# Query feature sums ahead of one more copy on the vector engine, their transposes issued as items of their own

## The chip, the cores and the metric

The kernel runs on one core of a Trainium2 chip. The metric is the device time of one execution in microseconds (us), as the median of several runs. A core has five engines that each work through their own instructions in order and wait for each other through semaphores: TensorE (PE, matmuls; PEld is its weight load), VectorE (DVE), ScalarE (ACT), GpSimd (POOL) and SyncE (SP, which here issues nearly all DMAs).

## The reference

Two attention branches share one input x of 2048 rows and 640 columns (32 heads of 20) and are mixed by a gate per row.

```python
g = sigmoid((x * gate_w).sum(-1, keepdims=True))
return g * A(x) + (1 - g) * B(x)
```

Branch A is linear attention with softmax features. Branch B cuts the rows into four segments of 512. In each it takes causal softmax attention within the segment and adds, by a weight per head, a read of a memory that all earlier segments have filled:

```python
phi = lambda t: jnp.where(t > 0, t + 1.0, jnp.exp(t))
for s in range(4):
    a_dot = softmax(qs @ ks.T * scale + mask) @ vs
    pq = phi(qs)
    a_mem = (pq @ M) / (pq @ z + 1e-6)
    outs.append(g * a_mem + (1 - g) * a_dot)
    pk = phi(ks)
    M, z = M + pk.T @ vs, z + pk.sum()
```

The features phi(q) of the queries are what the change is about. Segment 0 needs none, since the memory is empty.

## The kernel before, in words

The first 144 us compute branch A up to its normalised rows and the projections of segment 0 for branch B. The rest of the kernel is branch B and the output product. All five engines are on a manual schedule there: the order in which the code emits instructions is the order on each engine, and the order is written out by hand.

**Steps.** The loop over `dstep` makes 16 steps, four to a segment; "step s.d" is step d of segment s, each counted from 0. A step treats two groups of four heads, a and b. It emits five *bursts*: a burst is eight matmuls into two PSUM tiles `st_ps` (L621), each turned into probabilities `PT` by an exponential on ACT (L625), and then masked on POOL by triangular selects (L632). Between the bursts the step emits *items*, a list that the strings in `PLAN` spell out, one letter per item:

- `h`: half a projection (five matmuls, L804, into a PSUM tile `proj`, and a DVE copy, L810) of keys, queries or values of the next segment. After the second half of a key or query chunk follow its transpose on SP (L520) and an entry in the list of features to come.
- `f`, `o`: half an output row block (`f`) or half of branch A's part of one (`o`): matmuls L755 into a `proj` tile and a DVE copy into `orow` or `oTA` (L766).
- `A`, `D` and `B`, `C`: the products of probabilities and values (L677) into the PSUM tile `nda`, `A` and `D` for group a of this step, `B` and `C` for group b of the step before. `D` and `C` end with the memory read (L685), the memory update (L690) and the epilogue `emit_epi` on DVE and POOL: `rec` (L702, L704), `td` (L714; L710 in segment 0), `mtmp` (L720), then on POOL `oB` (L717), `Msb` (L723) and `Mbd` (L724).
- `x`, `y`: the sums that finish one chunk of features, `x` for keys, `y` for queries.
- `t`, `u`: transposes of finished rows on SP.

An item is emitted when the work of the items so far falls behind the share of the bursts; items of no weight, such as `x` and `y`, go with the item before them.

**Features.** phi is made in two parts. `exps` (L780) takes the exponential on ACT into `ek`, after the first burst for queries and after the third for keys. `rest` holds the sums: on DVE a minimum with 1 in place (L783) and the sum with max(x, 0) (L784). For keys that is all. For queries the sum goes to one staging tile `phiq_st` (a part of a tile that the profile calls Eq), and two transposes on SP (L789) follow at once, which bring it into place in `xTf`.

**Buffers that matter here.** `proj` has two PSUM banks that all halves (`h`, `f`, `o`) take in turn: a half can begin when the copy of the half before last has ended. `nda` has one buffer: `A` and `B` begin after the epilogue of the group before. `st_ps` has two tiles, `ek` two buffers, `phiq_st` one.

**Order in a step of segment 2**, as the string `hhBhhyCfhhxADt` gives it: two key halves, `B`, two query halves, the query sums with their transposes (`y`), `C` with its epilogue, an output half, two value halves, the entry `x`, `A`, `D`, a row transpose.

Of the kernel before, what the change touches and what calls it, by code (L numbers as in the profile page):

```python
# [15 lines left out]
def kernel(  # L16
# [15 lines left out]
    nc = tc.nc  # L32
    P = 128
# [266 lines left out]
    for n in range(KC):  # L300
        emit_foldM(WkT, WkA, n)
        if n in (1, 3):
            for sc in (n - 1, n):
# [4 lines left out]
                          in_=gw_ps[:, :, None, None].to_broadcast([P, KC, 2, 1]))  # L308
# [15 lines left out]
    for n in range(KC):  # L324
# [10 lines left out]
        out=xg, in0=vA[:, :, 0, 320].rearrange("p (g u) -> p u g", u=4)[:, :, :, None].to_broadcast([P, 4, 4, 4]),  # L335
# [192 lines left out]
    for ch in range(NCH):  # L528
# [8 lines left out]
        part, c = (("k", ch // 4), ("q", ch // 4), ("v", ch // 4), ("v", 4 + ch // 4))[k]  # L537
# [33 lines left out]
    with ExitStack() as bctx:  # L571
# [16 lines left out]
        xr = xTf.rearrange("p (r u) -> p r u", u=L)  # L588
        HOMES = {1: ((0, 6, 0), (6, 8, 1)), 2: ((0, 3, 9), (3, 8, 2)), 3: ((0, 6, 0), (6, 8, 1))}
        phiq_st = Eqf[:, 2 * G * L:2 * G * L + 2 * L].rearrange("p (h e) -> p h e", e=32)  # L590
# [44 lines left out]
        def bursts(a, b):  # L635
            out = []

            def add(name, parts, at):
                PT = bpt.tile([P, 4, L], BF16, name=name)

                def burst():
                    by_pairs = at if name == "PT1" and parts[0][0].last else ()
                    emit_burst(parts, PT, by_pairs)
                    if not by_pairs:
                        triangles(PT, at)
                out.append(burst)
                return PT

            for st in (a, b):
                st.PT[0] = add("PT0", ((st, 0, 0),), (0,))  # L650
                st.PT[1] = add("PT1", ((st, 3, 384), (st, 1, 0)), (0, 3))
                if st is a:
                    PT = add("PT2", ((a, 2, 0), (b, 2, 256)), (0, 2))
                    a.PT[2], b.PT[2] = (PT, 0), (PT, 256)
            return out
# [13 lines left out]
        def pv_items(st, js):  # L669
            vB = vBs[st.s % 2]  # L670

            def piece(j, i):
                if j == 0 and i == 0:
                    st.nda = bnd.tile([P, 2, 512], F32, name="nda")
                nd = st.nda[:, 0, 0:4 * GP].rearrange("p (j i e) -> p j i e", j=4, i=4)
                for c in range(j + 1):
                    nc.tensor.matmul(nd[:, j, i], lhsT=block(st, c)[:, i, (j - c) * P:(j - c + 1) * P],  # L677
                                     rhs=vB[:, c, 4 * st.g + i, :], start=(c == 0), stop=(c == j))
            return [(0.026 * (j + 1), lambda j=j, i=i: piece(j, i)) for j in js for i in range(4)]

        def mem_items(st):
            g = st.g

            def am(j):
                nc.tensor.matmul(st.nda[:, 1, j * GP:(j + 1) * GP], lhsT=phiq_block(st.s, g, j),  # L685
                                 rhs=Mbd[:, g].rearrange("p i e -> p (i e)"), start=True, stop=True)

            def mz(c):
                Mz = st.nda[:, 1, 4 * GP:5 * GP].rearrange("p (i e) -> p i e", i=4)
                nc.tensor.matmul(Mz, lhsT=phiks[st.s % 2][:, c, 4 * g:4 * g + 4, :],  # L690
                                 rhs=vBs[st.s % 2][:, c, 4 * g:4 * g + 4, :],
                                 start=(c == 0), stop=(c == 3))
            return ([(0.037, lambda j=j: am(j)) for j in range(4) if st.s > 0]
                    + [(0.037, lambda c=c: mz(c)) for c in range(4) if st.s < NSEG - 1]
                    + [(0.0, lambda: emit_epi(st))])
# [30 lines left out]
        def emit_oT(ch):  # L726
            oT = bw.tile([P, KC, P], BF16, name="oT", bufs=4)
            nc.sync.dma_start_transpose(out=oT, in_=oBs[ch // 4][:, ch % 4])
            oTs[ch] = oT
# [40 lines left out]

        waiting = {"k": [], "q": []}
        sums = {"k": [], "q": []}

        def features(part, sc):
            src = stages[part][sc % 2][:, :, 0:DH]
            dst = phiks[(sc // 4) % 2][:, sc % 4] if part == "k" else phiq_st

            def exps():
                ek = bw.tile([P, H, DH], BF16, name="ek")
                nc.scalar.activation(out=ek, in_=src, func=ACT.Exp)  # L780

                def rest():
                    nc.vector.tensor_scalar_min(out=ek, in0=ek, scalar1=1.0)  # L783
                    nc.vector.scalar_tensor_tensor(out=dst[:, :, 0:DH], in0=src, scalar=0.0,  # L784
                                                   in1=ek, op0=ALU.max, op1=ALU.add)
                    if part == "q":
                        c = sc % 4
                        for g0, g1, r in HOMES[sc // 4]:
                            nc.sync.dma_start_transpose(  # L789
                                out=xr[:, r:r + 4 * (g1 - g0 - 1) + 1:4, c * P:(c + 1) * P],  # L790
                                in_=phiq_st[:, 4 * g0:4 * g1].rearrange("p h e -> p (h e)"))
                sums[part].append(rest)
            waiting[part].append(exps)

        def run_first(fns):
            if fns:
                fns.pop(0)()
# [19 lines left out]
        def half_items(s, order):  # L817
            return [half_item(part, 4 * s + c, half) for part, c in order for half in range(2)]
# [9 lines left out]

        PLAN = {0: ("hhhhhhxAhD", "hhBhyhChoxAoD", "hoBhoyChoxAoD", "hoBooyCooxAoD"),
                1: ("hhBhhyChhxADtt", "hhBhhyCfhhxAD", "hhBhhyCfhhxADt", "hhBhhyCfhhxAD"),
                2: ("hhBhhyCfhhxADt",) * 4,
                3: ("fBfyCffADtt", "ftBfCftfAD", "fBfCftfAD", "ufBfCfffAD")}

        oT4 = oTA[:, 0:4]

        def turn_last(n):
            nc.sync.dma_start_transpose(out=oT4[:, n, 0:3], in_=oBs[NSEG - 1][:, n, 0:3 * P])

        prev = None
        for dstep in range(NSEG * G // 2):
            s, gd = divmod(dstep, G // 2)
            if gd == 0 and s + 1 < NSEG:
                halves = half_items(s + 1, FIRST_SEG if s == 0 else CHUNKED)
            a, b = Step(2 * dstep), Step(2 * dstep + 1)
            items = []
            for w in PLAN[s][gd]:
                if w in "hfo":
                    items += {"h": halves, "f": fins, "o": aouts}[w].pop(0)  # L850
                elif w in "xy":
                    items.append((0.0, lambda part="kq"[w == "y"]: run_first(sums[part])))
                elif w == "u":
                    items += [(0.0, lambda n=n: turn_last(n)) for n in range(4)]
                elif w == "t":
                    items.append((0.0, lambda ch=turns.pop(0): emit_oT(ch)))
                else:
                    st = a if w in "AD" else prev
                    items += pv_items(st, (0, 1, 2)) if w in "AB" else pv_items(st, (3,)) + mem_items(st)
            share = sum(w for w, _ in items) / 5  # L860
            done = 0.0
            for n, burst in enumerate(bursts(a, b)):
                burst()
                if n in (0, 2):
                    run_first(waiting["kq"[n == 0]])
                while items and (n == 4 or done + items[0][0] / 2 < (n + 1) * share):
                    w, fn = items.pop(0)
                    fn()
                    done += w
            prev = b  # L870
# [93 lines left out]
```

## Time and profile before

| what | value |
|---|---|
| median of 3 runs | 344.57 us (344.26 to 344.86) |
| the profiled execution | 343.32 us |
| its span in the profile | 341.6 us |
| PE busy | 316.6 us, 93% |
| ACT busy | 259.9 us, 76% |
| DVE busy | 222.7 us, 65% |
| POOL busy | 206.4 us, 60% |
| granted TensorE clock | 1.00 |
| steps of segment 0 | 143.8 to 188.2 us |
| steps of segment 1 | 188.2 to 235.5 us |
| steps of segment 2 | 235.5 to 283.7 us |
| steps of segment 3 and the end | 283.7 to 341.6 us |

The page of the profile gives busy time by engine, and in 40 equal slices of the span, where each digit is the busy share in tenths (9 is 90% or more). The table of waits names for each engine and line the idle time before it and the event that came last before it began: total us, times, longest. The event is inferred; where the engine named had long been done, it was another. A timeline lists instructions in order of time: start in us, duration in us, engine, line, operation, output, input, size, how many were merged, and in brackets the idle time of the engine before, with what ended it. The ends of matmuls are modelled.

### The profile page before, as it was taken

To read this page: it belongs to the slowest core of one execution; us is meant where nothing else is said; L and a number is where in the kernel's file an instruction comes from. 1 tells how busy PE (TensorE), PEld (TensorE's weight loads), DVE (VectorE), ACT (ScalarE), POOL (GpSimd) and SP (SyncE) were. 2 spreads that over 40 slices of the span, in tenths; PEclk is the share of its full clock that TensorE was granted. 3 is DMA by queue.
4 is the path that set the end of the run, shared out by engine and by line. 5 is a ranking of instruction groups with operands and counts; after the bars stand their busy time and mean duration, and the time that the engine had idled before them with its cause. 6 is when DMAs were issued, how large, how long until landed. Compare 5 with 4: busy or idle time off the path is not lost.

```text
span 341.6 us, 9744 instructions
## 1 busy us (share of the span) xinstructions
PE 316.6 (93%) x4021; PEld 218.8 (64%) x4021; DVE 222.7 (65%) x448; ACT 259.9 (76%) x331; POOL 206.4 (60%) x301
## 2 busy tenths in 40 slices
PE   7999999989969999889988999999999999999994
PEld 6788888874437777645555556565555556665672
DVE  2466886479779889547676568667565664544552
ACT  4888887508855345699999988898888889889842
POOL 8177688500407888846566666757666666666550
PEclk9999999999999999999999999999999999999999
DMA  8839969895006778854433373543664551431222
GB/s 237 268 72 180 120 97 116 124 306 187 0 2 60 98 125 119 140 98 87 54 63 64 41 113 75 74 91 63 111 77 84 109 86 49 90 79 46 40 80 77
DMA packets 83381, 34.21 MB, mean 100 GB/s; under 512 B 69258, under 2 KB 83338, under 8 KB 83338
## 3 DMA queue, kind: packets, MB, share of 16 engines
q1 hardware_dynamic: 82906, 33.11, 52.6%
q8 instruction: 31, 0.51, 0.7%
q10 hardware_dynamic: 432, 0.49, 0.5%
q14 instruction: 12, 0.10, 0.1%
HBM read 9.21 MB, written 2.62 MB: 35 GB/s over the span
## 4 chain that ended last, share of the span: by engine, by line
PE 47%; ACT 21%; DVE 17%; issue 7%; POOL 5%; DMA 3%; SPq 0%; ACTq 0%; DVEq 0%; POOLq 0%
ACT PT L625 18%; PE st_ps L621 7%; PE pk L214 6%; PE pv L214 6%; PE proj L755 5%; PE proj L804 4%; PE nda L677 4%; PE pq L265 4%; PE proj L506 3%; DVE tt L454 3%; DVE Eq L784 3%; PE num L410 2%; DVE rr L432 2%; DVE td L714 2%; DVE zz L251 2%
## 5 line engine op out<-in xcount | busy, mean ns | idle before, releaser
L625 ACT ACTIVATE PT<-st_ps 128x1024 bf16<-128x1024 f32 x160 | 154.1, 1024 | 19.2 <-PE st_ps L621 11.7
L632 POOL TENSOR_SCALAR_AFFINE_SELECT PT<-PT 128x512 bf16<-128x512 bf16 (+1 forms) x130 | 84.9, 671 | 51.7 <-ACT PT L625 51.4
L226 POOL TENSOR_TENSOR EkSn<-Ek,krec 128x1280 bf16<-128x1280 bf16 x16 | 37.7, 2362 | 18.0 <-DVE krec L225 16.3
L677 PEld LDWEIGHTS <-PT 128*128 128x128 bf16 x1280 | 39.9, 96 | 12.0 <-issue 7.3
L677 PE MATMUL nda<-vB,PT 128*128 128x21 bf16 x1280 | 42.8, 173 | 1.6 <-DVE mtmp L720 1.2
L810 DVE CAST Z<-proj 128x320 bf16<-128x320 f32 x48 | 22.9, 488 | 32.2 <-PE proj L804 32.0
L804 PEld LDWEIGHTS <-xTf 128*128 128x128 bf16 x320 | 28.0, 97 | 21.5 <-issue 12.8
L214 PEld LDWEIGHTS <-xTf 128*128 128x128 bf16 x320 | 35.3, 113 | 7.1 <-ACT xTf L192 0.3
L222 DVE TENSOR_REDUCE ksum<-Ek 128x64 f32<-128x1280 bf16 x16 | 23.6, 1478 | 12.4 <-ACT Ek L218 12.4
L270 ACT ACTIVATE Eq<-pq 128x1024 bf16<-128x1024 f32 x20 | 19.4, 1021 | 13.0 <-PE pq L265 13.0
L454 DVE TENSOR_TENSOR tt<-num,rr 128x640 f32<-128x640 f32 x32 | 25.2, 813 | 5.2 <-PE num L410 2.7
L755 PE MATMUL proj<-WkA,oTA 128*128 128x320 bf16 x160 | 27.3, 299 | 0.0
L621 PE MATMUL st_ps<-Z 32*128 32x512 bf16 (+3 forms) x256 | 23.4, 299 | 4.2 <-ACT PT L625 2.1
L545 POOL TENSOR_TENSOR oA<-tt 128x640 bf16<-128x640 f32 x16 | 24.6, 1544 | 4.0 <-DVE tt L454 3.2
L218 ACT ACTIVATE Ek<-pk 128x640 bf16<-128x640 f32 x32 | 20.8, 701 | 7.8 <-PE pk L214 5.4
L717 POOL TENSOR_TENSOR oB<-td 128x320 bf16<-128x320 f32 x23 | 19.8, 862 | 11.4 <-DVE td L714 8.4
L410 PEld LDWEIGHTS <-Eq 128*128 128x128 bf16 x384 | 20.2, 96 | 9.4 <-issue 5.7
L621 PE MATMUL st_ps<-Eq 32*128 32x512 bf16 (+3 forms) x256 | 24.5, 299 | 1.8 <-ACT PT L625 0.9
L214 PE MATMUL pv<-WvA,xTf 128*128 128x321 bf16 x160 | 24.6, 300 | 0.0
L214 PE MATMUL pk<-WkA,xTf 128*128 128x320 bf16 x160 | 24.4, 299 | 0.2 <-ACT xTf L192 0.2
L755 PE MATMUL proj<-WvA,oT 128*128 128x320 bf16 x120 | 22.6, 300 | 0.0
L265 PE MATMUL pq<-xTf,WqA 128*128 128x512 bf16 x100 | 22.1, 379 | 0.0
(142 smaller groups left out, 544.4 us busy)
## 6 DMA issues: line engine op xcount, KB each, us to landing
Z<-EkSn SPq DMA_DIRECT2D x32, 160.0 KB, 4.9
x_nat<-in_A_x_dram SPq DMA_DIRECT2D x8, 320.0 KB, 6.6
out_dram<-orow SPq DMA_DIRECT2D x10, 160.0 KB, 2.0
WvA<-in_A_wqkv_dram SPq DMA_DIRECT2D x2, 400.0 KB, 6.0
wnat_q<-in_A_wqkv_dram SPq DMA_DIRECT2D x1, 800.0 KB
WkB<-in_B_wk_dram SPq DMA_DIRECT2D x1, 800.0 KB, 7.3
WqB<-in_B_wq_dram SPq DMA_DIRECT2D x1, 800.0 KB, 9.1
WvB<-in_B_wv_dram SPq DMA_DIRECT2D x1, 800.0 KB, 10.7
```

What stands on the lines that cost most here:

```text
L214: nc.tensor.matmul(ps[:, bk, 0:n], lhsT=xTk[:, c, sc // 4, sc % 4], rhs=rhs, start=(c == 0), stop=(c == KC - 1))
L226: nc.gpsimd.tensor_tensor(out=EkSn[:, sc].rearrange("p s (h f) -> p (s h) f", f=DH), in0=Ek.rearrange("p s (h f) -> p (s h) f", f=DH), in1 ...
L265: nc.tensor.matmul(pq[:, half, :], lhsT=WqA[:, c, j * P:(j + 1) * P], rhs=xT[:, c, t0:t0 + 512], start=(c == 0), stop=(c == KC - 1))
L410: nc.tensor.matmul(ps(bk, lo, hi), lhsT=Eqs[qb, j][:, sgn, qc * P:(qc + 1) * P], rhs=kvx[:, sgn, j, lo - h0:hi - h0, :].rearrange("p h e - ...
L454: nc.vector.tensor_tensor(out=tt[:, sgn].rearrange("p (b h) d -> p b h d", b=2), in0=ps, in1=csb, op=ALU.mult)
L545: nc.gpsimd.tensor_tensor(out=oA.rearrange("p (h d) -> p h d", d=DH), in0=tt[:, 0], in1=tt[:, 1], op=ALU.add)
L621: nc.tensor.matmul(ps[:, i - i0, o:o + L - c * P], lhsT=kT[32 * i:32 * i + 32, c * P:(c + 1) * P], rhs=qT[32 * i:32 * i + 32, c * P:L], st ...
L625: nc.scalar.activation(out=PT[:, i0:i0 + 2], in_=ps, func=ACT.Exp, scale=SCALE_B)
L632: nc.gpsimd.affine_select(out=v, in_=v, pattern=[[0, n_i], [1, P]], compare_op=ALU.is_ge, fill=0.0, base=0, channel_multiplier=-1)
L677: nc.tensor.matmul(nd[:, j, i], lhsT=block(st, c)[:, i, (j - c) * P:(j - c + 1) * P], rhs=vB[:, c, 4 * st.g + i, :], start=(c == 0), stop= ...
L755: nc.tensor.matmul(ps, lhsT=oT[:, k % KC], rhs=W[:, k % KC, hs], start=(k == 0), stop=(k == n - 1))
L804: nc.tensor.matmul(ps, lhsT=xT[:, k, sc * P:(sc + 1) * P], rhs=W[:, k, half * 320:(half + 1) * 320], start=(k == 0), stop=(k == KC - 1))
```

## The change

The query sums `y` move forward in the strings of `PLAN`, and the two transposes that followed them become an item `z` of their own, which stays behind the query half. `rest` no longer issues the transposes; it puts a function that does so into the list `q_turns`, and `z` runs the oldest one.

```diff
+        q_turns = []
 
         def features(part, sc):
...
                     if part == "q":
-                        c = sc % 4
-                        for g0, g1, r in HOMES[sc // 4]:
-                            nc.sync.dma_start_transpose(
-                                out=xr[:, r:r + 4 * (g1 - g0 - 1) + 1:4, c * P:(c + 1) * P],
-                                in_=phiq_st[:, 4 * g0:4 * g1].rearrange("p h e -> p (h e)"))
+                        q_turns.append(turn)
+
+                def turn():
+                    c = sc % 4
+                    for g0, g1, r in HOMES[sc // 4]:
+                        nc.sync.dma_start_transpose(
+                            out=xr[:, r:r + 4 * (g1 - g0 - 1) + 1:4, c * P:(c + 1) * P],
+                            in_=phiq_st[:, 4 * g0:4 * g1].rearrange("p h e -> p (h e)"))
...
-        PLAN = {0: ("hhhhhhxAhD", "hhBhyhChoxAoD", "hoBhoyChoxAoD", "hoBooyCooxAoD"),
-                1: ("hhBhhyChhxADtt", "hhBhhyCfhhxAD", "hhBhhyCfhhxADt", "hhBhhyCfhhxAD"),
-                2: ("hhBhhyCfhhxADt",) * 4,
-                3: ("fBfyCffADtt", "ftBfCftfAD", "fBfCftfAD", "ufBfCfffAD")}
+        PLAN = {0: ("hhhhhhxAhD", "hhBhyhzChoxAoD", "hoBhyozChoxAoD", "hoBoyozCooxAoD"),
+                1: ("hhBhyhzChhxADtt", "hhBhyhzCfhhxAD", "hhBhyhzCfhhxADt", "hhBhyhzCfhhxAD"),
+                2: ("hhBhyhzCfhhxADt",) * 4,
+                3: ("fByfzCffADtt", "ftBfCftfAD", "fBfCftfAD", "ufBfCfffAD")}
...
                     items.append((0.0, lambda part="kq"[w == "y"]: run_first(sums[part])))
+                elif w == "z":
+                    items.append((0.0, lambda: run_first(q_turns)))
```

Line numbers after the change are one to six higher from here on: the sums are L784 and L785, the projection copy L814, the query feature transposes L793.

## The prediction

> **What bounds the kernel now.** I read the page first, then the table of waits, then the chain of one step, then the timelines of DVE and PE side by side. Times inside a step are from step 2.2 (third step of segment 2, 262 to 274 us) unless another is named. The page's shares of the span:
>
> ```profile
> PE 316.6 (93%) x4021; PEld 218.8 (64%) x4021; DVE 222.7 (65%) x448; ACT 259.9 (76%) x331; POOL 206.4 (60%) x301
> PE   7999999989969999889988999999999999999994
> ACT  4888887508855345699999988898888889889842
> ```
>
> From slice 17 on (144 us, where the steps begin) PE and ACT are both nearly full and DVE is not. So DVE can only matter where PE or ACT waits for it. The waits say where:
>
> ```profile
> ACT PT L625 <- POOL Mbd L724: 5.9, 7, 0.9
> PE proj L804 <- DVE orow L766: 3.7, 7, 0.5
> PE nda L677 <- DVE mtmp L720: 1.2, 2, 0.6
> ```
>
> Columns: total us, times, longest. The seven PE waits stand in steps 1.1 to 1.3 and 2.0 to 2.3, the two others in steps 0.2 and 0.3. The chain of waits runs through the sums in each of these nine; one step of it:
>
> ```profile
> 266.14 0.82 DVE Eq L784
> ...
> 267.61 0.84 DVE td L714
> ```
>
> DVE Eq L784 is the query sum, td the product behind it. Now DVE and PE around them:
>
> ```profile
> 263.76 0.49 DVE L810 CAST Z<-proj 128x320 bf16<-128x320 f32 x1 [1.22 <-PE proj L804]
> 265.36 0.49 DVE L810 CAST Z<-proj 128x320 bf16<-128x320 f32 x1 [1.10 <-PE proj L804]
> 265.77 0.34 DVE L783 TENSOR_SCALAR ek<-ek 128x640 bf16<-128x640 bf16 x1
> 266.14 0.82 DVE L784 SCALAR_TENSOR_TENSOR Eq<-Z,ek 128x640 bf16<-128x640 bf16 x1
> 266.89 0.35 DVE L702 RECIPROCAL rec<-nda 128x32 f32<-128x32 f32 x1
> ...
> 268.51 0.48 DVE L766 CAST orow<-proj 128x320 bf16<-128x320 f32 x1
> ```
> ```profile
> 265.71 0.31 PE L690 MATMUL nda<-vB,Z 128*128 128x84 bf16 x4
> ...
> 267.10 0.72 PE L755 MATMUL proj<-WvA,oT 128*128 128x320 bf16 x4
> 267.65 0.84 PE L804 MATMUL proj<-WvB,xTf 128*128 128x320 bf16 x5
> 269.04 0.57 PE L804 MATMUL proj<-WvB,xTf 128*128 128x320 bf16 x3 [0.55 <-DVE orow L766]
> 269.54 0.40 PE L621 MATMUL st_ps<-Z 32*128 32x128 bf16 x8
> ```
>
> PE finishes nda at 266.02, but DVE still has the sums (L783, L784) ahead of rec and gets there at 266.89. Everything behind slips: td, mtmp, then the orow copy, which ends at 268.99. `proj` has two banks, so the second value half needs the bank that orow empties; PE starts it at 269.04, 0.05 after. Behind it in PE's order is the step's fifth burst (269.54), so ACT, done with the fourth at 269.20, starts at 270.06. The page names POOL Mbd for that idle time; but the buffer ACT writes there was last touched by POOL a step earlier, and the burst's end (269.94) fits, so I take PE as the releaser. By the other reading POOL's work also follows td and comes as much earlier, so the gain is the same.
>
> In the same excerpt DVE idles 1.10 us between the two query copies. The sums take 266.89 - 265.77 = 1.12 us from start to next start.
>
> **The change, part by part.** Nothing is added or removed; the instructions of PE, ACT, POOL and SP stand in the same order. On DVE the pair L783+L784 moves ahead of one copy in eleven steps: 0.2 and 0.3 (past an oTA copy), 1.0 to 1.3 and 2.0 to 2.3 (past the second query copy), 3.0 (past an orow copy). In step 0.1 it stays. The two transposes of each query feature chunk keep their place in SP's queue behind the queries' own transpose, which is what `z` is for.
>
> *Does the pair wait in its new place?* It needs ek from ACT, which ended at 262.74 (row 262.00, 0.74) against a start at 263.76+0.41 = 264.17: 1.4 us spare; in 0.2, 0.3, 1.0 and 1.1 the same subtraction leaves 1.4 to 1.8. It also overwrites the staging tile that the previous step's transposes read; these were issued 12 us before and land 2.8 us after issue. So it does not wait.
>
> *Steps 1.1 to 1.3 and 2.0 to 2.3.* New order: copy 263.76, pair 264.17 to 265.29, copy at 265.36 as before, ending 265.85. rec starts when nda is ready, 266.02+0.04 = 266.06 instead of 266.89 (DVE starts 0.04 after PE's end, as the copy at 265.36 does): 0.83 earlier. td and mtmp keep their distance, so DVE is free for the orow copy at 268.51 - 0.83 = 267.68; what is late next is the output half itself, whose matmuls end at 267.82. The copy runs 267.86 to 268.35, PE is released at 268.40 instead of 269.04: 0.64. In step 1.1 (half ends 207.65, PE restarted at 208.80) the same working gives 208.80 - 208.23 = 0.57. Lower bounds are the idle rows alone (0.55, 0.54, 0.47), upper bounds the start-to-start values, since a following matmul starts about 0.15 before the modelled end of the one before; I take the upper, as starts are recorded and ends modelled. Sum 6 x 0.64 + 0.57 = 4.4 (at least 3.7). ACT's gap of 0.85 shrinks to about 0.2 and stays above zero, so PE's gain passes through.
>
> *Steps 0.2 and 0.3.* Here PE waits for mtmp, as nda has one buffer:
>
> ```profile
> 171.52 0.49 DVE L766 CAST oTA<-proj 128x320 bf16<-128x320 f32 x1 [1.27 <-PE proj L755]
> 174.44 0.60 PE L677 MATMUL nda<-vB,PT 128*128 128x21 bf16 x18 [0.62 <-DVE mtmp L720]
> ```
>
> The 1.27 us idle hold the pair; rec comes at 172.07 instead of 173.02, mtmp 0.95 earlier, and PE's wait is gone. ACT idled 0.69 there and gives no more than that: 0.62 to 0.69 each, together 1.3.
>
> *Step 1.0.* No orow copy. PE waits 0.23 us at 199.29 for the query feature transposes, issued at 196.34 right after L784; the queries' own transpose occupies SP to 196.11, so they can come 0.2 earlier: 0 to 0.23, I take 0.15. *Step 3.0.* DVE idled 2.99 us before the pair and PE waited for nothing behind it: 0.
>
> *What it costs.* The pair now meets the POOL selects at 264.71. L784 ran 824 ns alone and up to 1251 in its twelve query runs: at most 0.43, which pushes the second copy to 265.72 and rec to 266.13, 0.07 later than in the sum. The output half covers 267.86 - 267.68 = 0.18 of that, so it costs nothing; without the cover it would be 0.07 a step. The select that loses (1.90 for two at 172.29 against 1.23) is needed only by value products five us later. The later second copy delays the queries' transpose by at most 0.3; the last of a segment is issued near 278.0, lands 3.2 later, and is read at 283.68: covered.
>
> Sum 4.4 + 1.3 + 0.15 = 5.85, bounds 3.7 + 1.24 = 4.9 and 6.0. The profiled execution took 343.32 (span 341.6 and 1.7 around it), which makes 337.5; the median of the runs is 1.25 above it, so 344.57 - 5.85 = 338.7.
>
> **The rivals.**
> *ACT takes over (partial gain).* By windows ACT is busy 93% of segment 0, 91% of segment 1, 86% of segment 2. If its remaining gaps in the first two cannot be given up, only 4 x 0.64 remains: 2.6, 342.0. For it: that share. Against: the gaps (0.69, 0.85) stand exactly where PE was stalled.
>
> *The pair is locked out (slower).* If L784 loses against both selects in a row (264.71 + 1.22), it starts at 265.93, the second copy at 266.68, rec at 267.09 instead of 266.89: 0.20 in nine steps, 1.8, so 346.4. It turns to a loss once L784 is held over 1.19 us. Against: where they met before (195.12, select from 195.00) it ran 1.19, 0.37 more, and a second select did not hold it. The Trainium skill, "SBUF — State Buffer", section "Who interferes with whom", says a DVE instruction with two SBUF inputs and a GpSimd instruction that reads SBUF exclude each other, the later one blocked until the first is through. By that rule one select held is possible, two only if the second wins the port again; the trace's 1.19 agrees with one.
>
> *Nothing changes.* If PE's releaser is misnamed like ACT's, 344.6. Against: the 0.05 between the orow copy and PE in all seven.
>
> **How the numbers follow.** Forecast 0.77 (338.5 to 339.7), ACT partial 0.09 (342.0), no change 0.05, locked out or an unseen wait of that kind 0.09. About 0.2% (0.7 us) is what a measurement here can tell from no change. The range 337.8 to 342.0 holds the first two cases and, below, 0.7 for a gap of ACT or PE that I have not seen. Faster 0.86, same 0.05, slower 0.09.
>
> **What would show it.** After: the row PE proj <- DVE orow falls from 3.7 to under 0.7; PE nda <- DVE mtmp vanishes; DVE's idle time before the second query copy falls from 1.10 to about 0.1; rec follows nda within 0.1; steps of segment 2 shorten from 12.1 to 11.5 us. It is wrong if the second query copy starts over 0.5 us after its matmuls, or if an equal wait of PE for ACT appears in segments 0 and 1.

## The result, and the profile after

The changed kernel takes 340.83 us (median of 4 runs, 340.22 to 341.03), the kernel before, on the same chip, 344.54 (4 runs, 344.26 to 344.86). The ratio is 0.9877, with a 95% interval of 0.9848 to 0.9907: 3.7 us faster. The forecast was 338.7, in a range of 337.8 to 342.0.

The two profiled executions are 343.32 and 340.92, which is only 2.4 apart, because the first 144 us, which the change does not touch, differ: the first exponential of the steps stands at 144.23 before and 145.55 after, and from 97 to 102 us the granted clock is 1.00 before and 0.67 after. So from here on the steps alone are compared. A step's length is the time from its first exponential (L625) to the first of the next step; all steps and the end together took 197.37 us before and 193.62 after, 3.75 less, which is the gain of the medians. Step 0.1, whose order on DVE no edit changes, takes 11.16 or 11.17 in both kernels and in the runs e1, e5, e6, e7 and e12 below.

| step | before | after | gain | predicted |
|---|---|---|---|---|
| 0.2, 0.3 | 11.32, 11.37 | 11.16, 11.16 | 0.37 | 1.3 |
| 1.0 | 11.38 | 11.12 | 0.26 | 0.15 |
| 1.1 | 11.74 | 11.79 | -0.05 | 0.57 |
| 1.2, 1.3 | 12.11, 12.12 | 11.55, 11.55 | 1.11 | 1.28 |
| 2.0, 2.1, 2.3 | 12.10, 12.04, 12.11 | 11.55, 11.51, 11.51 | 1.68 | 1.92 |
| 2.2 | 11.88 | 11.70 | 0.18 | 0.64 |
| 3.0 | 11.61 | 11.37 | 0.24 | 0 |

The page after has the same picture, with PE and ACT a little fuller:

```profile
PE 317.5 (94%) x4021; PEld 219.2 (65%) x4021; DVE 224.8 (66%) x448; ACT 259.6 (77%) x331; POOL 209.2 (62%) x301
...
PE   6899999989978999988999999999999999999994
...
ACT  4888887508845455689999999999889889889842
```

In the table of waits after, the row of PE `proj` for DVE `orow` is gone (3.7 before), and what stands under POOL Mbd is down from 5.9. ACT's wait for the bursts has grown from 11.7 to 13.2, and a wait of PE for `mtmp` is still there:

```profile
ACT PT L625 <- PE st_ps L621: 13.2, 31, 1.2
...
PE st_ps L621 <- ACT PT L625: 2.9, 11, 0.5
...
ACT PT L625 <- POOL Mbd L724: 1.3, 6, 0.2
...
PE nda L677 <- DVE mtmp L720: 0.8, 3, 0.5
```

DVE's timeline in step 2.2 after (the lines are one to four numbers higher now). The pair L784, L785 stands ahead of the second query copy, `rec` starts when `nda` is ready, and the `orow` copy is no longer what PE waits for:

```profile
262.43 0.49 DVE L814 CAST Z<-proj 128x320 bf16<-128x320 f32 x1 [1.26 <-PE proj L808]
262.84 0.32 DVE L784 TENSOR_SCALAR ek<-ek 128x640 bf16<-128x640 bf16 x1
263.19 0.83 DVE L785 SCALAR_TENSOR_TENSOR Eq<-Z,ek 128x640 bf16<-128x640 bf16 x1
264.03 0.49 DVE L814 CAST Z<-proj 128x320 bf16<-128x320 f32 x1
264.73 0.36 DVE L702 RECIPROCAL rec<-nda 128x32 f32<-128x32 f32 x1 [0.21 <-PE nda L690]
...
266.52 0.49 DVE L766 CAST orow<-proj 128x320 bf16<-128x320 f32 x1
```

PE and ACT over the end of the same step (the last fence is ACT before the change, the fifth burst and the next step's first in one row):

```profile
266.32 1.31 PE L808 MATMUL proj<-WvB,xTf 128*128 128x320 bf16 x8
267.56 0.75 PE L621 MATMUL st_ps<-Z 32*128 32x128 bf16 x8
...
269.94 0.52 PE L621 MATMUL st_ps<-Z 32*128 32x512 bf16 x4
```
```profile
265.93 1.94 ACT L625 ACTIVATE PT<-st_ps 128x1024 bf16<-128x1024 f32 x2 [0.69 <-PE st_ps L621]
268.08 1.94 ACT L625 ACTIVATE PT<-st_ps 128x1024 bf16<-128x1024 f32 x2 [0.21 <-POOL Mbd L724]
270.43 1.94 ACT L625 ACTIVATE PT<-st_ps 128x1024 bf16<-128x1024 f32 x2 [0.41 <-PE st_ps L621]
```
```profile
270.06 3.94 ACT L625 ACTIVATE PT<-st_ps 128x1024 bf16<-128x1024 f32 x4 [0.86 <-POOL Mbd L724]
```

The eight value matmuls run through, where before they broke after five. But the fifth burst, 0.40 before, now takes 0.75: its second tile `st_ps` is still being read by ACT's exponential, which ends at 267.87. PE has come too early by 0.35 (0.75 less 0.40). And ACT, which went from the fifth burst to the next step's first with hardly a break before (0.07), now waits 0.41 there. The table of waits hides PE's part, as it lies inside a merged row; it is seen in the row's duration.

### The profile page after: what moved, and what is told of

Read it like the earlier page. It is cut to its first block, busy times and chain, and to the rows that moved or that the text cites. A ratio compares the mean times of both kernels' runs of the same rounds, so it can differ in the third digit from the quotient of the medians.

```text
span 339.2 us, 9735 instructions
## 1 busy us (share of the span) xinstructions
PE 317.5 (94%) x4021; PEld 219.2 (65%) x4021; DVE 224.8 (66%) x448; ACT 259.6 (77%) x331; POOL 209.2 (62%) x301
## 4 chain that ended last, share of the span: by engine, by line
PE 61%; ACT 17%; DVE 10%; DMA 6%; issue 4%; POOL 1%; SPq 0%; ACTq 0%; DVEq 0%
ACT PT L625 15%; PE st_ps L621 10%; PE proj L755 9%; PE nda L677 7%; PE pk L214 6%; PE pv L214 6%; PE proj L808 6%; PE pq L265 5%; PE proj L506 3%; DVE tt L454 3%; DMA x_nat<-in_A_x_dram 2%; PE num L410 2%; DVE zz L251 2%; DVE rr L432 2%; DMA Z<-EkSn 1%
## 5 line engine op out<-in xcount | busy, mean ns | idle before, releaser
L625 ACT ACTIVATE PT<-st_ps 128x1024 bf16<-128x1024 f32 x160 | 154.4, 1025 | 15.9 <-PE st_ps L621 13.2
L632 POOL TENSOR_SCALAR_AFFINE_SELECT PT<-PT 128x512 bf16<-128x512 bf16 (+1 forms) x130 | 86.9, 687 | 48.0 <-ACT PT L625 47.9
L677 PEld LDWEIGHTS <-PT 128*128 128x128 bf16 x1280 | 39.8, 96 | 11.6 <-issue 8.4
L814 DVE CAST Z<-proj 128x320 bf16<-128x320 f32 x48 | 22.8, 486 | 22.6 <-PE proj L808 22.1
L621 PE MATMUL st_ps<-Z 32*128 32x512 bf16 (+3 forms) x256 | 24.9, 299 | 4.1 <-ACT PT L625 2.1
L621 PE MATMUL st_ps<-Eq 32*128 32x384 bf16 (+3 forms) x256 | 24.8, 299 | 1.4 <-ACT PT L625 0.8
L265 PE MATMUL pq<-xTf,WqA 128*128 128x512 bf16 x100 | 23.1, 392 | 0.0
```

The source lines that it names most:

```text
L265: nc.tensor.matmul(pq[:, half, :], lhsT=WqA[:, c, j * P:(j + 1) * P], rhs=xT[:, c, t0:t0 + 512], start=(c == 0), stop=(c == KC - 1))
L621: nc.tensor.matmul(ps[:, i - i0, o:o + L - c * P], lhsT=kT[32 * i:32 * i + 32, c * P:(c + 1) * P], rhs=qT[32 * i:32 * i + 32, c * P:L], st ...
L625: nc.scalar.activation(out=PT[:, i0:i0 + 2], in_=ps, func=ACT.Exp, scale=SCALE_B)
L632: nc.gpsimd.affine_select(out=v, in_=v, pattern=[[0, n_i], [1, P]], compare_op=ALU.is_ge, fill=0.0, base=0, channel_multiplier=-1)
```

## The experiments

Two theories were set up. *Handshake*: `st_ps` has two tiles, PE fills both in a burst and ACT empties both, so PE and ACT wait for each other in turn, and a stall of PE is worth only what exceeds the wait for ACT that takes its place. *Lock*: DVE's instructions with two SBUF inputs and POOL's selects hold each other up, and the change alters who meets whom. Runs without a spread were taken once. Unless an edit says otherwise, it is to the changed kernel.

### The change in segment 0 alone (e1)

```diff
-  1: ("hhBhyhzChhxADtt", ...), 2: ("hhBhyhzCfhhxADt",) * 4, 3: ("fByfzC...
+  1: ("hhBhhyzChhxADtt", ...), 2: ("hhBhhyzCfhhxADt",) * 4, 3: ("fBfyzC...
```

> Only the strings of segment 0 are those of the change; segments 1 to 3 keep the order of before (sums and transposes behind the second query half). The first burst starts 0.2 and 0.3 begin are compared by step length (from the first exponential of a step to the first of the next). Theory 'two-tile handshake' (what PE gains before the fifth burst it partly loses waiting for ACT to free the second st_ps tile, and ACT then idles about 0.41 us at the next step's first burst): steps 0.2 and 0.3 take 11.16 us instead of 11.32 and 11.37, together 0.37 less; 1.1 to 2.3 stay at 11.7 to 12.1. Rival 'sum as predicted' (the 0.69 us gap of ACT is fully recovered, and something later took it back): 10.7 each, 1.3 less in total.

Measured: steps 0.2 and 0.3 are 11.16 and 11.17 as in the changed kernel, steps 1.1 to 3.0 those of before within 0.01, but for 2.2 (12.11 here, 11.88 before). The time was 343.18. So steps 0.2 and 0.3 give 0.36, not 1.3, and the gains of the steps behind don't hang on them, with two exceptions. Step 1.0 takes 11.21 here, so 0.17 of its 0.26 comes with the order in segment 0. And step 2.2, with the order of before, is 0.23 longer than before: L704 meets another select there and takes 0.67 instead of 0.19 (see e5 and e12).

### More or less of PE's work ahead of a burst (e2, e3, e8, e4)

The step puts its items behind burst n until their work reaches the share; a shift moves matmuls from behind a burst to ahead of it.

```diff
+        SHIFT = (0, 0, 0, 0.3)      # e2; e3: -0.3; e8: 0.15; e4: (0, 0, -0.4, 0)
...
-  while items and (n == 4 or done + items[0][0] / 2 < (n + 1) * share):
+  while items and (n == 4 or done + items[0][0] / 2 < (n + 1) * share + SHIFT[n]):
```

> The changed kernel with 0.3 us more items emitted ahead of the fifth burst of every step (two projection matmuls of the second value half in segments 1 and 2). Theory 'two-tile handshake': PE waits 0.35 us inside the fifth burst for ACT, and this wait takes the two matmuls (0.28 us) for nothing, so that the next first burst comes earlier; ACT starts the fifth burst 0.1 to 0.3 later, so half is left: steps 1.2 to 2.3 take 11.4 instead of 11.5, 0.1 to 0.2 less each, in all 0.7 to 1.5 us. Rival 'lock' (VectorE against GpSimd for the shared port sets the steps) and rival 'ACT takes over': steps unchanged within 0.05.

> The changed kernel with 0.3 us fewer items ahead of the fifth burst (two matmuls go behind it). Theory 'two-tile handshake': PE comes to the burst 0.28 earlier, waits 0.28 longer for ACT, and ACT's idle time at the next first burst grows from 0.41 to about 0.7: steps 1.2 to 2.3 take 11.8, 0.28 more each; segment 0 likewise, 3 us in all. Rivals 'lock' and 'ACT takes over': unchanged within 0.05 a step.

> The changed kernel with 0.15 us more items ahead of the fifth burst (one matmul in segments 1 and 2, against two in the run with 0.3). Theory 'handshake': with none moved TensorE waits 0.35 in the fifth burst, with two it waits 0.28 in the next first burst and ScalarE 0.48 before the fifth, so one matmul lies between: steps 1.2 to 2.3 take 11.37 instead of 11.51 to 11.55; segment 0 takes 11.05 to 11.1 a step instead of 11.16. In all 1.2 to 1.6 us faster than the changed kernel, near 339.4. Rival 'something else holds the steps at 11.51': 11.5 as with two, and a total between those of none and two.

> The changed kernel with 0.4 us fewer items ahead of the fourth burst (three output matmuls go behind it). In segment 2 ACT idles 0.65 to 0.69 us before the fourth burst. Theory 'two-tile handshake': ACT does the fourth burst 0.4 earlier there, has freed both tiles when PE comes to the fifth, PE's wait of 0.35 is gone, and steps 2.0 to 2.3 take 11.2 instead of 11.5; in segment 1 ACT is busy with the key exponential until the fourth burst, so there the change is within 0.1. Rivals: segment 2 unchanged within 0.05.

| kernel | time, us | 0.2 | 1.1 | 1.2 | 2.0 | 2.2 | steps in all |
|---|---|---|---|---|---|---|---|
| changed | 340.83 | 11.16 | 11.79 | 11.55 | 11.55 | 11.70 | 193.62 |
| e2, two matmuls ahead of burst 5 | 339.57 (339.39 to 340.21) | 11.00 | 11.27 | 11.52 | 11.51 | 11.52 | 192.01 |
| e8, one ahead of burst 5 | 340.85 (340.56 to 342.03) | 11.01 | 11.38 | 11.61 | 11.61 | 11.57 | 192.89 |
| e3, two back behind burst 5 | 344.68 (one run) | 11.47 | 11.78 | 11.83 | 11.82 | 11.79 | 197.65 |
| e4, three back behind burst 4 | 342.62 (342.10 to 343.92) | 11.29 | 11.47 | 11.73 | 11.72 | 11.73 | 194.96 |

Against the kernel before, e2 has a ratio of 0.9836 (0.9817 to 0.9855), e8 0.9882 (0.9846 to 0.9917), e4 0.9926 (0.9901 to 0.9951).

In e3 PE reaches the fifth burst two matmuls sooner, waits longer in it, and the two matmuls stand behind it, where ACT waits for them: 0.27 to 0.28 longer in steps 1.2 and 2.0, 0.31 in 0.2, which is the price of two matmuls (two of 0.14), and what the theory expected. The edit leaves the order on DVE as it is, so PE's time before and behind a burst is not exchangeable. e2 takes PE's wait out of the fifth burst, and it comes back in the first of the next step (PE's timeline of e2):

```profile
255.05 0.47 PE L621 MATMUL st_ps<-Z 32*128 32x128 bf16 x8
...
256.88 0.39 PE L621 MATMUL st_ps<-Z 32*128 32x512 bf16 x2
257.55 0.39 PE L621 MATMUL st_ps<-Z 32*128 32x512 bf16 x2 [0.28 <-ACT PT L625]
```

So the regular steps come no lower than 11.51, and with one matmul (e8) PE waits at both places (rows of 0.61 and 0.79 where 0.40 is the free time) and they are 11.6. The 11.4 that the theory expected of both did not come, nor e8's 339.4. e4 was expected to gain and lost: its fourth burst waits for ACT inside (0.65), and the three matmuls behind it delay the fifth, ahead of which ACT idles 0.88. PE's wait in the fifth burst did go (0.40), but the steps of segment 2 are 11.7 instead of the 11.2 expected: the wait moved to the fourth.

e2 has the lowest time, 339.57. It was not timed in rounds beside the changed kernel, and its interval and the changed kernel's overlap at the edge, but its steps are shorter by 1.61. Of these 0.85 lie in segment 0, 0.52 in step 1.1 and 0.18 in step 2.2. In the last two L704 takes 0.34 and 0.19 instead of 0.65 and 0.56, so there it is the lock that e2 avoids, by the timing and not by intent.

### Without the selects: the lock (e5, e12)

```diff
-                nc.gpsimd.affine_select(out=v, in_=v, ...)
+                pass
```

e5 does this to the changed kernel, e12 to the kernel before.

> The changed kernel without GpSimd's triangular selects in branch B: the causal mask is left out, so VectorE meets GpSimd only in the epilogues. Theory 'handshake, with the lock in single places': steps 1.2, 1.3, 2.0 and 2.3 stay at 11.5 within 0.05, and the places where VectorE ran into a select recover: in step 1.1 the multiplication at L704 takes 0.19 instead of 0.65, TensorE's wait of 0.52 for mtmp is gone and the step takes 11.3 to 11.55 instead of 11.79; step 2.2 takes 11.5 instead of 11.70. Rival 'lock sets the steps': all of 1.1 to 2.3 get shorter by 0.2 or more. Rival 'no lock': 1.1 stays at 11.8.

> The kernel before without branch B's triangular selects (the causal mask inside a block is left out), the counterpart of e5, so that the change is seen once with nothing on POOL that could hold the pair or the small product L704. Two shares (ACT's handshake takes what segment 0 lost, the lock what steps 1.1 and 2.2 lost): this kernel keeps its steps of 12.1 us in segments 1 and 2 and of 11.3 to 11.4 in steps 0.2 and 0.3, so against e5 the change is worth 0.6 in every one of the steps 1.1 to 1.3 and 2.0 to 2.3, step 1.1 included, and still only 0.16 to 0.21 in steps 0.2 and 0.3: about 4.8 in the sum, where the full kernels showed 3.75. Rival (the lock is no part of it): step 1.1 differs by less than 0.1 and the sum stays at 3.75. Rival (the lock is all of it): 0.6 in steps 0.2 and 0.3 too, 5.8 in the sum.

| step | before | e12 | after | e5 | gain with selects | gain without |
|---|---|---|---|---|---|---|
| 0.2, 0.3 | 22.69 | 22.32 | 22.32 | 22.32 | 0.37 | 0.00 |
| 1.1 | 11.74 | 11.67 | 11.79 | 11.51 | -0.05 | 0.16 |
| 1.2 | 12.11 | 11.77 | 11.55 | 11.51 | 0.55 | 0.26 |
| 2.2 | 11.88 | 11.77 | 11.70 | 11.51 | 0.18 | 0.26 |
| 3.0 | 11.61 | 11.36 | 11.37 | 11.37 | 0.24 | 0.00 |
| all | 197.37 | 194.53 | 193.62 | 192.78 | 3.75 | 1.75 |

(Times of single runs: e5 340.62, e12 343.26; the steps of e12 begin at 147.02, 2.8 later than those of before.)

This was the largest surprise. The expectation for e12 was 4.8 in the sum, by the theory of two shares (the handshake and the lock); its rivals said 3.75 and 5.8. It came to 1.75, so all three are wrong. The selects cost the kernel before 2.84 and the changed kernel 0.84: 2.0 of the 3.75 gained are not the stall that the prediction priced, but delays by the selects that reach PE no longer.

The groups of DVE show the lock itself. The small product L704 (L703 in e12), 32 times, before, after and in e12:

```profile
L704 DVE TENSOR_TENSOR rec<-rec,Eq 128x32 f32<-128x32 f32 (+1 forms) x32 | 10.5, 328 | 1.3
```
```profile
L704 DVE TENSOR_TENSOR rec<-rec,Eq 128x32 f32<-128x32 f32 (+1 forms) x32 | 10.8, 336 | 1.3
```
```profile
L703 DVE TENSOR_TENSOR rec<-rec,Eq 128x32 f32<-128x32 f32 (+1 forms) x32 | 6.0, 187 | 1.3
```

It takes 187 ns when no select runs and up to 0.67 us otherwise. The Trainium skill, "SBUF — State Buffer", section "Who interferes with whom", says that a DVE instruction with two SBUF inputs contends with a GpSimd instruction that reads SBUF, by an exclusive lock. The trace agrees: L704 has two (`rec` and the gate weights in Eq), and in both kernels, wherever it takes 0.23 or more, it ends within 0.05 after the end of a select that ran beside it. The sum of its delays is about the same before and after (4.5 and 4.8). What differs is where they fall and who waits. The kernel before shows it by itself, in two of its steps. In step 2.2, L704 is free and the ten key matmuls take 1.37 from their start to that of `B`, which needs `mtmp` (DVE and PE, timelines of before):

```profile
260.18 0.19 DVE L704 TENSOR_TENSOR rec<-rec,Eq 128x32 f32<-128x32 f32 x1
```
```profile
260.48 1.53 PE L804 MATMUL proj<-WkB,xTf 128*128 128x320 bf16 x10
261.85 0.40 PE L677 MATMUL nda<-vB,PT 128*128 128x21 bf16 x10
```

In step 2.3, two selects run from 272.06 for 1.22, L704 is held, and the same stretch of PE takes 1.60:

```profile
272.07 0.67 DVE L704 TENSOR_TENSOR rec<-rec,Eq 128x32 f32<-128x32 f32 x1
```
```profile
272.37 1.53 PE L804 MATMUL proj<-WkB,xTf 128*128 128x320 bf16 x10
273.97 0.40 PE L677 MATMUL nda<-vB,PT 128*128 128x21 bf16 x10
```

PE loses 0.23 there, and the steps are 11.88 and 12.11: 0.23 again. Step 2.2 of before was short for lack of a collision, and after the change it has one (L704 0.56, step 11.70), which explains its small gain. After the change the regular steps lose little this way, for two reasons. L704 at their start is held less, 0.23 to 0.33 where it took 0.49 to 0.67 before. And what is left counts less: in step 2.3 after, `B` comes 1.60 behind the first key matmul, as in 2.3 before, and 1.39 behind it in e5, yet the step takes 11.51 after and in e5. PE's second burst shows why (first line after, second e5; 0.40 is the free time):

```profile
272.32 0.49 PE L621 MATMUL st_ps<-Z 32*128 32x128 bf16 x8
```
```profile
272.06 0.70 PE L621 MATMUL st_ps<-Z 32*128 32x128 bf16 x8
```

The delay takes the place of a wait for ACT inside that burst. In steps 0.2 and 0.3, where L704 takes more after the change than before (0.58 instead of 0.32 in the epilogue of `C`), they are 11.16 with and without selects.

Step 1.1 after is the collision at its worst: DVE, POOL and PE.

```profile
200.84 0.65 DVE L704 TENSOR_TENSOR rec<-rec,Eq 128x32 f32<-128x32 f32 x1
```
```profile
200.23 1.22 POOL L632 TENSOR_SCALAR_AFFINE_SELECT PT<-PT 128x512 bf16<-128x512 bf16 x2 [1.20 <-ACT PT L625]
```
```profile
202.65 0.40 PE L677 MATMUL nda<-vB,PT 128*128 128x21 bf16 x10 [0.52 <-DVE mtmp L720]
```

L704 ends 0.04 after the selects, `mtmp` is late, PE waits 0.52. Without selects (e5) the step is 11.51, and in e6, with all selects in place, L704 takes 0.22 there and the step is 11.51 too. Step 2.2 is 11.70 with L704 at 0.56, and 11.52 in e7 with 0.38. So in these two steps the cost goes with the held L704, not with POOL's work by itself.

And the handshake shows in e12's segment 0, PE's timeline in step 0.2:

```profile
176.98 0.62 PE L676 MATMUL nda<-vB,PT 128*128 128x21 bf16 x18 [0.38 <-DVE mtmp L719]
```

PE waits 0.38 here for `mtmp`, and the step is 11.16, exactly that of e5, whose order has no such wait. A wait of PE of 0.38 is free there. In segment 2 of e12, five value matmuls and the copy take 1.31 from start to restart (280.19 to 281.50) where five alone take 0.70: 0.61 lost. Taking that away (e5) is worth 0.26. The missing 0.35 is PE's wait in the fifth burst, which in e5 has 0.75 as in the changed kernel (PE in step 2.3 of e12, then of e5):

```profile
280.19 0.84 PE L803 MATMUL proj<-WvB,xTf 128*128 128x320 bf16 x5
281.50 0.57 PE L803 MATMUL proj<-WvB,xTf 128*128 128x320 bf16 x3 [0.47 <-DVE orow L765]
282.00 0.40 PE L621 MATMUL st_ps<-Z 32*128 32x128 bf16 x8
```
```profile
279.03 0.75 PE L621 MATMUL st_ps<-Z 32*128 32x128 bf16 x8
```

e5 and e12 leave out POOL's work too, not only its reads; what of the 2.84 is the lock alone is separated only in the steps named above.

### Shorter exponentials (e9, e10)

```diff
-  nc.scalar.activation(out=PT[:, i0:i0 + 2], in_=ps, func=ACT.Exp, scale=SCALE_B)
+  nc.scalar.activation(out=PT[:, i0:i0 + 2, P:L], in_=ps[:, :, P:L], func=ACT.Exp, scale=SCALE_B)
...
+  src = PT[:, i0:i0 + n_i, P:2 * P] if n == 0 else v
-  nc.gpsimd.affine_select(out=v, in_=v, ...)
+  nc.gpsimd.affine_select(out=v, in_=src, ...)
```

> The changed kernel, with each exponential L625 over three quarters of its columns (the first 128 of each 512 are left out, and the selects of those columns read the next 128), so ACT has about 0.22 us less for each of ten exponentials a step. To be set against e10, the kernel before with the same cut. Handshake theory: with ACT out of the way PE no longer waits for a free st_ps tile, steps of segments 1 and 2 are PE's work alone, about 11.2 us, those of segment 0 about 11.0; and the order of the sums is worth its whole predicted price: 0.6 to 0.65 more in e10 in steps 0.2, 0.3, 1.2, 1.3, 2.0 to 2.3, in the sum 5.3 to 5.9. Rival (the shortfall is the pair and the selects in each other's way, ACT has no part in it): e10 minus e9 stays at what the two kernels show with whole exponentials, 0.16 to 0.21 in segment 0 and 0.56 in segments 1 and 2, 3.75 in the sum.

> The kernel before with the same shorter exponentials as e9. Handshake theory: steps of segment 2 about 11.85 us, PE waits 0.55 to 0.6 for the orow copy in seven steps and 0.6 for mtmp in steps 0.2 and 0.3 as before, and each of these waits is a whole loss against e9. Rival: steps 0.2 and 0.3 longer than those of e9 by only 0.2.

Measured: 331.43 with the changed order (e9), 331.24 with the old one (e10), one run each; steps in all 183.75 and 184.85. Neither theory foretold that. By steps, e10 minus e9: 0.47 in 0.2 and in 0.3 (0.16 and 0.21 with whole exponentials), -0.92 in 1.0, -0.83 in 1.1, 0.97 in 2.1, 0.18 or 0.19 in the other five of segments 1 and 2. The selects come at other times here, and in e9 they hit the pair and L704 in nearly every step (DVE's timeline of e9, 1.13 and 0.53 where 0.83 and 0.19 are the free times):

```profile
258.54 1.13 DVE L786 SCALAR_TENSOR_TENSOR Eq<-Z,ek 128x640 bf16<-128x640 bf16 x1
...
260.38 0.53 DVE L705 TENSOR_TENSOR rec<-rec,Eq 128x32 f32<-128x32 f32 x1
```

So the stall is not gone in e9, as the handshake theory had taken for granted that it would be. PE's rows in step 0.2 and in step 2.2, e10 first, e9 second:

```profile
172.42 0.60 PE L678 MATMUL nda<-vB,PT 128*128 128x21 bf16 x18 [1.01 <-DVE mtmp L721]
...
262.06 0.57 PE L805 MATMUL proj<-WvB,xTf 128*128 128x320 bf16 x3 [0.54 <-DVE orow L767]
```
```profile
173.24 0.60 PE L678 MATMUL nda<-vB,PT 128*128 128x21 bf16 x18 [0.54 <-DVE mtmp L721]
...
262.44 0.57 PE L809 MATMUL proj<-WvB,xTf 128*128 128x320 bf16 x3 [0.35 <-DVE orow L767]
```

PE waits 0.47 longer in e10 in the first and 0.19 longer in the second, and in step 2.1 it waits 1.15 against 0.18. The steps differ by the same amounts, 0.47, 0.19 and 0.97, and the fifth burst takes its free 0.40 in both kernels in these steps. With whole exponentials a wait of 0.38 gave nothing (e12 and e5). That is the handshake's sign: once ACT is out of the way, what PE waits longer is what the step is longer.

Step 1.0 shows a cost of the change that the kernel itself doesn't pay. The second query copy stands behind the lengthened pair, so the queries' own transpose ends late and the feature transposes behind it in SP's queue are issued 0.57 later in the step than in e10 (7.33 against 6.76 after its first exponential), while PE gets there 0.31 sooner. It waits 1.25 for the last of them (0.34 in e10):

```profile
196.75 0.21 PE L686 MATMUL nda<-Mbd,xTf 128*128 128x84 bf16 x1 [1.25 <-DMA xTf<-Eq]
```

In step 1.1 of e9 the granted clock is 0.90, against 1.00 in e10, and its ten key matmuls take 2.80 instead of 1.53, so neither this step nor the totals can be compared:

```profile
197.68 2.80 PE L809 MATMUL proj<-WkB,xTf 128*128 128x320 bf16 x10
```

### Half bursts (e11)

Each burst is cut into its two tiles, with a tenth of the items behind each.

```diff
-  share = sum(w for w, _ in items) / 5
+  share = sum(w for w, _ in items) / 10
-                out.append(burst)
+                out.append(lambda: burst(0))     # heads 0, 1 of a group
+                out.append(lambda: burst(2))     # heads 2, 3
```

> The changed kernel with each burst cut into its two tiles, a tenth of the items behind each half: PE asks for a tile when it is free, and ACT has one tile to work on while PE fills the other. Handshake theory: PE's waits inside bursts and ACT's gaps ahead of them (0.2 to 0.7 each) go for the most part, steps of segments 1 and 2 come to about 11.2 us and of segment 0 to about 10.9, in all some 3.5 under the changed kernel: 337.3. Rival (the steps are bound by the lock and by PE's own work, not by the handshake): no shorter than 11.5, 340.5 or more.

Measured: 349.56 (348.99 to 350.05, ratio to before 1.0135, 1.0111 to 1.0160), steps of segment 2 12.4. PE's waits inside bursts did go, but PE itself has more to do. Half a burst takes as long as a whole one. The fourth burst of a step, which has four matmuls, not eight, shows it (PE's timeline of e11, and the whole burst in the changed kernel):

```profile
244.76 0.39 PE L620 MATMUL st_ps<-Z 32*128 32x512 bf16 x2
...
246.00 0.39 PE L620 MATMUL st_ps<-Z 32*128 32x512 bf16 x2
```
```profile
265.44 0.39 PE L621 MATMUL st_ps<-Z 32*128 32x512 bf16 x4
```

The four heads of a group use 32 rows of PE each and run side by side: four matmuls in 0.33 from start to next start, two in 0.32. The Trainium skill, "TensorEngine Tiling (Array Packing)", section "Key Properties", says that such tiles work independently and in parallel; the rows agree. Halving a burst gives up half of that, at about 0.3 for each of five bursts (an estimate from these rows), more than the waits were. The expectation had overlooked it, and the run says nothing on how low the handshake could go.

### The turns, and the sums still earlier (e6, e7)

```diff
-                        q_turns.append(turn)
+                        turn()                   # e6
```
```diff
-  1: ("hhBhyhzChhxADtt", ...), 2: ("hhBhyhzCfhhxADt",) * 4
+  1: ("hhByhhzChhxADtt", ...), 2: ("hhByhhzCfhhxADt",) * 4      # e7
```

> The changed kernel, but the feature transposes are issued with the sums again (z does nothing): on SP they stand ahead of the queries' own transpose, which comes up to 2.5 us later. All theories: inside a segment nothing changes (steps 1.1 to 1.3 and 2.1 to 2.3 within 0.05), since the queries are needed only in the next segment. At the ends of segments the last query transpose is issued near 278 instead of 276 in the profile of the changed kernel and lands 3.2 later, against a first use at 281.5: 0 to 0.3 us lost at each of two boundaries (steps 2.0 and 3.0).

> In segments 1 and 2 the query sums stand one copy further forward still, ahead of both query copies. The exponential they read ends within 0.1 us of the place where they now stand. Theory 'handshake': what counts is only that the sums are out of the place between the last query copy and rec; steps 1.2 to 2.3 stay at 11.5 within 0.05. Rival 'lock': the pair now meets other selects, so steps change by 0.2 or more either way.

e6 took 341.81 (steps 194.19 in all, 0.57 over the changed kernel). It gains 0.16 in step 1.0 and 0.28 in 1.1, and loses 0.70 in step 1.3: the feature transposes come first in SP's queue, that of the last queries of the segment is issued behind them, and ACT waits 1.11 ahead of the first burst of segment 2, which reads it (SP, then ACT, in e6; that this transpose is the releaser fits its place, issued at 232.59 where the changed kernel has it issued before the features, but was not tried by itself):

```profile
229.17 3.33 SPq L793 DMA_TRANSPOSE xTf<-Eq  x2
232.59 1.26 SPq L520 DMA_TRANSPOSE Z<-Z  x1
```
```profile
236.26 1.94 ACT L625 ACTIVATE PT<-st_ps 128x1024 bf16<-128x1024 f32 x2 [1.11 <-PE st_ps L621]
```

So the item `z` is needed. The expectation had at most 0.3 at the end of a segment and 0.05 inside; steps 2.1 and 2.2 are 0.15 and 0.11 longer too, which was not followed. e7 took 341.07 with the steps of the changed kernel within 0.01, but for 2.2 (11.52 instead of 11.70; its L704 was held less, 0.38 instead of 0.56). One copy ahead is enough: the stall is gone already, and what is left does not hang on the sums.

## Why the prediction was right, and where it was not

**The stall and the order of DVE: right.** `rec` follows nda's end at once, the row of PE `proj` for `orow` is gone, regular steps of segment 2 went from 12.1 to 11.5. The row of PE `nda` for `mtmp` was to vanish and did not (0.8): it went from steps 0.2 and 0.3, and L704's hold made a new one of 0.52 in step 1.1.

**"ACT's gap of 0.85 shrinks to about 0.2 and stays above zero, so PE's gain passes through": the failed step.** The gap shrank to 0.21, as said. But one gap of ACT above zero doesn't mean that PE is the bound all round the step. PE, early at the fifth burst, waits 0.35 inside it for ACT's tile, and ACT waits 0.41 at the next first burst for PE's work behind. The prediction had named that sign for its failure (a wait of PE for ACT), and had it among the rivals as *ACT takes over*, but for segments 0 and 1 as wholes and read from busy shares. It holds inside every step, and takes 0.35 of 0.61 in segment 2 and all of a 0.38 wait in segment 0 (e5, e12). With shorter exponentials, where PE waits for no tile in the fifth burst, what PE waits longer for DVE is a whole loss (e9, e10).

**"It costs nothing" (the selects): wrong on both sides.** The changed kernel pays 0.84 for them, most of it in steps 1.1 (0.28) and 2.2 (0.19). The kernel before paid 2.84, which the prediction did not see: it looked for the pair in its new place only, not for L704 in the kernel as it was. A regular step's gain of 0.55 is then roughly the 0.64 of the stall, less 0.35 for the handshake, plus 0.23 for `mtmp`, which was held through L704 before, is held less now and no longer counts: 0.52.

**Terms.** Steps 0.2 and 0.3 were put at 1.3 and gave 0.37, all of it from the selects (0.00 without them). Step 1.0, put at 0.15, gave 0.26, and step 3.0, put at 0, gave 0.24; without selects both give 0.03 or less, so these hang on the selects as well. The regular steps 1.2, 1.3, 2.0, 2.1 and 2.3 gave 2.79 of 3.2. The sum was put at 5.85 and came to 3.75. That the time lies in the range is in part luck, two errors that offset each other: the order as priced is worth 1.75 with the selects out, and 2.0 came from where nothing was counted.

**The rivals.** The pair was not locked out: L785 took 1.25 at most, and in the steps looked at the copy behind it did not make `rec` later than before. What was locked out, in step 1.1, was L704.

What stays open: e5 and e12 are one profiled execution each, and but for steps 1.1 and 2.2 POOL's queue and the lock are not told apart in them. Which selects L704 meets can differ where the order is the same (step 2.2 before and in e1, 0.23 apart), so a single step of one execution is no better known than that.

## What to carry to other kernels

Where two engines pass a pair of buffers to and fro, price a stall of one by what exceeds the wait for the other that takes its place, and look for that wait at every hand-over of the loop, not only at the one behind the stall; a merged row that grows (0.40 to 0.75) shows it where the table of waits doesn't. Before a change that moves an instruction past another engine's, compare the durations of short instructions with their shortest runs, in the kernel as it is: 10.5 us where 6.0 would do is a cost that is already paid and that the change may move. And an experiment that frees one engine shifts all meetings of the others, so read it step by step, not by its total.

## What the runs showed of the hardware

A 0.19 us product of 32 columns can take 0.67 us when selects run on POOL: in step 1.1 after the change it begins while two of them run and ends 0.04 after the later one. Two matmuls on 32 rows each take PE as long as four side by side (0.32 and 0.33).
